# Weight blocks converted in pairs of 1024 columns, and a set order for VectorE's first work

## The chip, the cores and the metric

The kernel runs on one core of a Trainium2 chip. The metric is the device time of one execution in microseconds (us), the median of several runs. The engines of the core are named as in the profile: PE is TensorE (matrix products), DVE is VectorE, ACT is ScalarE, POOL is GpSimd, SP is SyncE, which only issues transfers here. PEld is the load of weights into TensorE.

## The reference, cut

```python
# attention: batch 8, 8 heads, 576 tokens, head dimension 64
kv = einsum('bhsd,bhse->bhde', k, v)
out = einsum('bhsd,bhde->bhse', q, kv)
rms = sqrt(mean(out * out, axis=-1, keepdims=True) + 1e-06)
x = (out / rms * g_norm)                  # -> 4608 tokens x 512
# first MLP, w_in 512 x 2048, w_out 2048 x 512
h = x @ w_in
x = (h * cos(h)) @ w_out
# second MLP, 512 -> 1024 -> 1024 -> 512
a, b = x @ w1, x @ w2
return ((a * b) @ w3) @ w_out
```

The weights come as float64 words, two 32-bit words a number. The kernel has to turn them into float32 itself.

## The kernel before, in words

Every product that needs full float32 accuracy is made of three products of rounded halves, hi x hi, hi x lo and lo x hi (`three`). So each operand is split: ScalarE copies it rounded (hi), VectorE or GpSimd subtracts that from the source (lo). That is `split`; a hi part always comes before its lo part, on another engine.

**The weights** come through the class `Chunk`, blocks of 128 x 512 numbers. A block is loaded as raw words on SP's queue (`load`), then `convert` makes float32 bits of it: one Abs on ScalarE (it only has to read the high words), and four VectorE operations: clamp (L139), shift and mask (L140), sign (L143) and the low word's bits (L146). Then `put` splits the result into the weight tile. A matrix step m of the first MLP needs one block of w_in (128 x 512, named i) and one of w_out (named u). `first_pairs` sets the order of these blocks and the buffers of their words: buffers of weights that are not there yet (tags wo8 to wo15), then bc. A load can only be issued when the buffer's last reader is done.

**The tokens** are cut into 16 units of 288 (two a batch entry) for attention, and into nine blocks t of 512 for the MLPs. `first_units` does units 0 and 1 by itself: for each of four head pairs p the product kv, the split of q, the product out, its square. A small matmul gathers the mean squares (`ms_first`), a Newton iteration on VectorE makes the inverse roots of all of them (L349 to L355: a start value and three rounds of three operations), a matmul with a unit matrix spreads them over the partitions (`spread`), and a multiply (L438) finishes o. Then `split_x` makes hi and lo parts of x of block t = 0.

All other units go through `unit_stage`, eleven stages s: loads of k, v and q, kv, out, mean square, then at s = 8 `emit_newton` (L349 to L355 on 128 x 18) and `emit_bc`: the inverse roots go to DRAM (rsd) and come back spread over the partitions (bc). At s = 10 `emit_x` multiplies (L383). Units 2 and 3, which make the x of block t = 1, are spread over the first seven steps by the table `quick`; their transfers go through GpSimd's queue (`queue`). They also need a trip through DRAM for the mean square (msd, then rsx).

**The steps.** The main loop runs over n; each step is a block t and a slice m of 128 of the 2048 hidden units. Steps 0 to 7 are t = 0 with m = 0 to 7, steps 8 to 23 are t = 1 with m = 0 to 15, steps 24 to 31 are t = 0 with m = 8 to 15, then t = 2 and so on. A step makes h (12 matmuls of 128 x 512, `emit_h`, h8 is that of step 8), then g = h cos h on ScalarE and VectorE (`g_first`: u, r, the rest; `g_rest`: sine, u x h, split), and two steps later g @ w_out is added up (`emit_w`, w5 is that of step 5). Two PSUM banks hold h; h of step n + 2 needs the bank of step n, which is free after the multiply u x h (L555).

**Who sets the order.** The code is written as a list per step, but a planner of the language orders each engine's instructions by a simulated timeline and puts in the waits. `tc.issue_after(op)` tells it not to place what follows before op. Every engine and each transfer queue then works strictly in the order that it was given.

Of the kernel before, what the change touches and what calls it, by code (L numbers as in the profile page):

```python
# [13 lines left out]
P = 128  # L14
EPS = 1e-6
# [19 lines left out]
def kernel(  # L35
# [47 lines left out]
    def wi_tile(m, name):  # L83
        return wpool.tile([P, 2, KD, P], F32R, tag=f"wi{m}", name=name)

    def wo_tile(m, name):
        return wpool.tile([P, 2, DM], F32R, tag=f"wo{m}", name=name)

# [25 lines left out]

    class Chunk:


        def __init__(self, name, src, tag, put):
            self.name, self.src, self.tag, self.put = name, src, tag, put

        def load(self):
            if self.tag == "stage":
                self.words = stage([P, CHUNK, 2], I32, f"{self.name}_w")
            elif self.tag == "bc":
                self.words = ap.tile([P, CHUNK, 2], I32, tag="bc", name=f"{self.name}_w")
            else:
                self.words = wpool.tile([P, CHUNK, 2], I32, tag=self.tag, name=f"{self.name}_w")
            word_loads.append(
                nc.sync.dma_start(out=self.words.rearrange("p n t -> p (n t)"), in_=self.src)
            )  # L130

        def convert(self):


            lo, hi = self.words[:, :, 0], self.words[:, :, 1]
            self.f = row(f"{self.name}_f")
            b = self.f.bitcast(I32)
            nc.scalar.activation(self.f, hi.bitcast(F32), AF.Abs)
            yield nc.vector.tensor_scalar(self.f, self.f, MOST, LEAST, ALU.min, ALU.max)  # L139
            yield nc.vector.tensor_scalar(  # L140
                b, b, 3, 0x3FFFFFF8, ALU.logical_shift_left, ALU.bitwise_and
            )
# [12 lines left out]
    def may_load():
        k = state["load"]
        if k >= len(chunks):
            return False
        tag = chunks[k].tag
        return tag == "stage" or last_words.get(tag, -1) < state["conv"]  # L160

    def prefetch(upto):
        while state["load"] < upto and may_load():
            c = chunks[state["load"]]
            c.load()
            last_words[c.tag] = state["load"]
            state["load"] += 1
# [27 lines left out]
    def put_w_in(m):  # L195
        def put(f):
            t = wi_tile(m, f"w_in{m}")
            split(t.rearrange("p i k f -> p i (k f)"), f)
            w_in[m] = t
        return put  # L200

    def put_w_out(m):
        def put(f):
            t = wo_tile(m, f"w_out{m}")
            split(t, f)
            w_out[m] = t
        return put

    def first_pairs():


        pairs = [(0, 0), (1, 0)]
        for m in range(2, NM):
            pairs += [(m, 0), (m - 2, 1)]
        pairs += [(NM - 2, 1), (NM - 1, 1)]
        free = list(range(NM // 2, NM))
        for m, s in pairs:
            if s == 1 and m in free:
                free.remove(m)
            tag = f"wo{free[0]}" if free else "bc"  # L220
            free = free[1:] + free[:1]
            nm, put = (("i", put_w_in), ("u", put_w_out))[s]
            src = w1pair[m, :, 2 * CHUNK * s:2 * CHUNK * (s + 1)]
            chunks.append(Chunk(f"{nm}{m}", src, tag, put(m)))

    first_pairs()
    n_first = len(chunks)
    for i in range(2 * NJ):
        chunks.append(Chunk(f"d{i}", w12w[i], "stage", put_later(("w12", i))))
    for c in range(NJ):  # L230
        chunks.append(Chunk(f"o{c}", wo2w[c], "stage", put_later(("wo2", c))))
    for half in range(2):
        for c in range(NJ):
            src = w3t[c, :, 2 * CHUNK * half:2 * CHUNK * (half + 1)]
            chunks.append(Chunk(f"a{half}{c}", src, "stage", put_later(("w3", half, c))))
# [53 lines left out]
    def load_q(u, p, tag=None):  # L289
        if tag:  # L290
            t = wpool.tile([P, HALF], F32, tag=tag, name=f"q_{u}_{p}")
# [55 lines left out]
    def newton(x, y, t):  # L347
# [41 lines left out]
    def first_units(spread):  # L389

        for p in range(NPAIR):
            emit_kv(0, p)
            evac_kv(0, p)
            for u in range(2):
# [3 lines left out]
                split(hl, q_raw.pop((u, p)), nc.vector)  # L398
# [17 lines left out]
                for k in range(NT3):  # L416
# [4 lines left out]
                    )  # L421
        n = 4 * NPAIR * NT3
        x, y, t = (row(f"rs_first_{i}")[0:T3, 0:n] for i in range(3))
        nc.vector.tensor_scalar(x, mst[0:T3, 0:n], EPS, HUGE, ALU.add, ALU.min)
        newton(x, y, t)
        for u in range(2):
            for p in range(NPAIR):
                ps = ps_acc.tile([P, 512], F32, tag=f"acc{p}", name=f"spread_{u}_{p}")
# [9 lines left out]
                nc.vector.tensor_tensor(o, o, ps[:, 0:HALF], ALU.mult)  # L438
# [102 lines left out]
    def g_first(n):  # L541
# [317 lines left out]
    if True:  # L859
# [8 lines left out]
        spread = wpool.tile([P, T3], F32, tag=f"wi{NM - 1}", name="spread")  # L868
# [19 lines left out]
        nc.vector.tensor_scalar(gneg, gneg, -1.0, None, ALU.mult)  # L888
        for p in range(NPAIR):
            for u in range(2):  # L890
                load_q(u, p, f"wi{4 + 2 * p + u}")
# [26 lines left out]
        for n in range(NS + 2):  # L918
# [7 lines left out]
            more = min(n_first, 9 + n + min(n, 8) // 2) - state["conv"] if n < NS else 0  # L926
# [12 lines left out]
            if n < NS:  # L939
                if more > 0:  # L940
                    put(more)
# [205 lines left out]
```

## Time and profile before

| | |
|---|---|
| time, median of 3 runs | 1544.08 us (1543.64 to 1544.95) |
| the profiled execution's own time | 1546.17 us |
| its span | 1544.40 us |
| mean granted clock of TensorE | 0.993 |
| busy, PE / DVE / ACT / POOL | 1500.9 / 924.8 / 697.5 / 371.4 us |
| share of the chain that ended last | PE 81%, DMA 5%, DVE 3%, POOL 3%, ACT 2% |

The span is the time between the first and the last instruction of the profiled execution; its own time has 1.77 us around that, and lies 2.09 us above the median of the runs. The busy times may overlap between engines. A busy time of one instruction is longer than the distance to the next one, since an engine starts the next before the last is written. In the timelines, square brackets give the idle time of the engine before the instruction and what ended it.

### The profile page before, as it was taken

To read this page: it belongs to the slowest core of one execution; us is meant where nothing else is said; L and a number is where in the kernel's file an instruction comes from. 1 tells how busy PE (TensorE), PEld (TensorE's weight loads), DVE (VectorE), ACT (ScalarE), POOL (GpSimd) and SP (SyncE) were. 2 spreads that over 40 slices of the span, in tenths; PEclk is the share of its full clock that TensorE was granted. 3 is DMA by queue.
4 is the path that set the end of the run, shared out by engine and by line. 5 is a ranking of instruction groups with operands and counts; after the bars stand their busy time and mean duration, and the time that the engine had idled before them with its cause. 6 is when DMAs were issued, how large, how long until landed. Compare 5 with 4: busy or idle time off the path is not lost.

```text
span 1544.4 us, 20537 instructions
## 1 busy us (share of the span) xinstructions
PE 1500.9 (97%) x7616; PEld 1272.0 (82%) x7616; DVE 924.8 (60%) x1714; ACT 697.5 (45%) x1405; POOL 371.4 (24%) x301
## 2 busy tenths in 40 slices
PE   6799999999999999999999998999999999999998
PEld 6577888788787787878887887999998998999997
DVE  3998844566566666766666447644544456545453
ACT  4667654444454454444534335433433334333331
POOL 1111010120010211101102006454444417344420
PEclk9799999999999999999999999999999999999999
DMA  8655120433333425234222015121102313223312
GB/s 288 218 158 159 43 71 7 150 111 110 113 97 97 146 97 153 87 108 132 88 73 92 11 40 192 42 82 69 69 28 82 110 59 113 78 93 123 123 62 75
DMA packets 81956, 156.26 MB, mean 101 GB/s; under 512 B 11600, under 2 KB 37376, under 8 KB 81856
## 3 DMA queue, kind: packets, MB, share of 16 engines
q1 hardware_dynamic: 80240, 150.18, 30.3%
q0 software_dynamic: 1616, 4.78, 1.0%
q8 instruction: 59, 0.97, 0.3%
q14 instruction: 41, 0.34, 0.1%
HBM read 113.77 MB, written 41.15 MB: 100 GB/s over the span
## 4 chain that ended last, share of the span: by engine, by line
PE 81%; DMA 5%; DVE 3%; POOL 3%; ACT 2%; issue 2%; SPq 0%; ACTq 0%; POOLq 0%; DVEq 0%
PE X L762 11%; PE h L529 8%; PE x L531 8%; PE x L530 8%; PE h L531 8%; PE h L530 8%; PE x L529 8%; PE V L762 5%; PE o L529 4%; PE o L530 4%; PE o L531 4%; PE Y L762 3%; POOL xc L112 2%; DMA x2r<-x_all 2%; PE kv L269 1%
## 5 line engine op out<-in xcount | busy, mean ns | idle before, releaser
L762 PE MATMUL X<-xc,w 128*128 128x384 f32 x1152 | 230.0, 337 | 6.6 <-ACT s L770 5.9
L531 PE MATMUL x<-g,w_out 128*128 128x512 f32 x576 | 227.6, 395 | 0.0
L530 PE MATMUL x<-g,w_out 128*128 128x512 f32 x576 | 227.1, 394 | 0.0
L529 PE MATMUL h<-x,w_in 128*128 128x512 f32 x544 | 216.3, 398 | 5.1 <-DVE u L555 3.4
L762 PEld LDWEIGHTS X<-xc,w 128*128 128x128 f32 x1152 | 204.0, 188 | 19.9 <-ACT s L770 9.9
L530 PE MATMUL h<-x,w_in 128*128 128x512 f32 x544 | 215.1, 395 | 1.8 <-DVE x L112 1.8
L531 PE MATMUL h<-x,w_in 128*128 128x512 f32 x544 | 215.0, 395 | 0.0
L529 PE MATMUL x<-g,w_out 128*128 128x512 f32 x576 | 212.7, 392 | 1.1 <-ACT g L110 0.6
L112 POOL TENSOR_TENSOR xc<-x2r,xc 128x768 fp32r<-128x768 f32 x70 | 134.6, 1930 | 225.2 <-ACT xc L110 225.2
L543 ACT ACTIVATE u<-h 128x512 f32<-128x512 f32 x144 | 86.2, 598 | 157.4 <-PE h L531 153.8
L554 ACT ACTIVATE u<-u 128x512 f32<-128x512 f32 x144 | 91.0, 632 | 121.6 <-DVE u L550 106.7
L112 DVE TENSOR_TENSOR g<-u,g 128x512 fp32r<-128x512 f32 x144 | 104.4, 725 | 64.6 <-ACT g L110 64.4
L110 ACT ACTIVATE g<-u 128x512 fp32r<-128x512 f32 x144 | 90.9, 632 | 109.1 <-DVE u L555 86.3
L112 POOL TENSOR_TENSOR qhl<-q,qhl 128x288 fp32r<-128x288 f32 x48 | 42.3, 884 | 397.7 <-ACT qhl L110 317.8
L529 PEld LDWEIGHTS h<-x,w_in 128*128 128x128 f32 x544 | 103.1, 190 | 33.0 <-DVE u L555 8.0
L530 PEld LDWEIGHTS x<-g,w_out 128*128 128x128 f32 x576 | 108.6, 189 | 24.6 <-DVE rs L353 0.5
L529 PEld LDWEIGHTS x<-g,w_out 128*128 128x128 f32 x576 | 107.6, 188 | 25.2 <-DVE x2s L576 0.8
L531 PEld LDWEIGHTS x<-g,w_out 128*128 128x128 f32 x576 | 108.8, 189 | 23.0
L555 DVE TENSOR_TENSOR u<-u,h 128x512 f32<-128x512 f32 x144 | 98.7, 685 | 47.3 <-ACT u L554 46.9
L549 DVE TENSOR_SCALAR r<-u 128x512 f32<-128x512 f32 x112 | 50.7, 453 | 127.3 <-ACT u L543 127.2
L770 ACT ACTIVATE s<-X 128x384 f32<-128x384 f32 x144 | 65.9, 487 | 133.6 <-PE X L762 133.2
L530 PEld LDWEIGHTS h<-x,w_in 128*128 128x128 f32 x544 | 103.1, 190 | 24.4 <-DVE x L112 2.5
(183 smaller groups left out, 2646.9 us busy)
## 6 DMA issues: line engine op xcount, KB each, us to landing
x2r<-x_all SPq DMA_DIRECT2D x44, 384.0 KB
kvraw<-in_kv_main_dram SPq DMA_DIRECT2D x28, 512.0 KB
x_all<-x2s SPq DMA_DIRECT2D x36, 256.0 KB
part<-o SPq DMA_DIRECT2D x36, 256.0 KB
part<-part SPq DMA_DIRECT2D x36, 256.0 KB
out_dram<-part SPq DMA_DIRECT2D x36, 256.0 KB
i_w<-in_w1pair_dram SPq DMA_DIRECT2D x16, 512.0 KB
u_w<-in_w1pair_dram SPq DMA_DIRECT2D x16, 512.0 KB
```

What stands on the lines that cost most here:

```text
L110: nc.scalar.activation(dst[:, 0], src, AF.Copy)
L112: lo_engine.tensor_tensor(dst[:, 1], src, f32(dst[:, 0]), ALU.subtract)
L269: nc.tensor.matmul(ps[d, 0:D], k[:, d], v[:, d], start=i == 0, stop=i == NC)
L529: nc.tensor.matmul(ps, w[0], x[0], start=first, stop=False)
L530: nc.tensor.matmul(ps, w[0], x[1], start=False, stop=False)
L531: nc.tensor.matmul(ps, w[1], x[0], start=False, stop=last)
L543: nc.scalar.activation(u, h_ps[n], AF.Identity, bias=0.25, scale=INV_2PI)
L549: nc.vector.tensor_scalar(r, u, ROUND, ROUND, ALU.add, ALU.subtract)
L554: nc.scalar.activation(u, u, AF.Sin, scale=-TWO_PI_DOWN)
L555: nc.vector.tensor_tensor(u, u, h_ps.pop(n), ALU.mult)
L762: nc.tensor.matmul(ps, w[:, self.i, a, k], x[:, b, k], start=first and k == 0 and n == 0, stop=last and k == 1 and n == 2, skip_group_chec ...
L770: nc.scalar.activation(s, ps, AF.Copy)
```

## The change

Blocks of w_in and w_out of one m are handled together, as a `Pair`: one load of 1 MB (1024 numbers of 64 bits a partition), one Abs, four VectorE operations of 1024 columns, one hi and one lo operation. The result is written into the high words of the raw buffer itself instead of a buffer of its own. The words of the first eight pairs lie where the weights of pairs 8 to 15 will be and all eight loads stand right behind those of q. Pair 15 is converted in two halves through the bc buffers.

`first_units` sets an order with `behind`: the four VectorE operations of pair 0 stand between the q splits, then Newton comes in one run, then pair 0 is split, then for each p the spread, the multiply, the split of x and the operations of pair 1. The quick units stand behind pair 1 (`marks[2]`), and the conversion of pair n + 2 in step n behind the last u of g (`marks[-1]`). In steps 7, 9 and so on to 21 the pairs 8 to 15 follow.

```diff
+    def bits(f, words, at):
+        lo, hi = words[..., 0], words[..., 1]
+        b, at = f.bitcast(I32), at.bitcast(I32)
+        nc.scalar.activation(f, hi.bitcast(F32), AF.Abs)
+        yield nc.vector.tensor_scalar(f, f, MOST, LEAST, ALU.min, ALU.max)
+        yield nc.vector.tensor_scalar(
+            b, b, 3, 0x3FFFFFF8, ALU.logical_shift_left, ALU.bitwise_and
+        )
+        yield nc.vector.scalar_tensor_tensor(
+            at, hi, -0x40000000, b, ALU.bitwise_and, ALU.bitwise_or
+        )
+        yield nc.vector.scalar_tensor_tensor(
+            at, lo, 29, at, ALU.logical_shift_right, ALU.bitwise_or
+        )
...
+    class Pair:
...
+        def load(self):
+            m = self.m
+            at = m + NM // 2 if m < NM // 2 else m + 1
+            self.raw = wpool.tile([P, 2 * CHUNK, 2], I32, tag=f"w{at}", name=f"words_{m}")
+            nc.sync.dma_start(out=self.raw.rearrange("p n t -> p (n t)"), in_=w1pair[m])
+
+        def convert(self):
+            f = wpool.tile([P, 2, CHUNK], F32, tag=f"w{self.m}", name=f"bits_{self.m}")
+            words = self.raw.rearrange("p (s n) t -> p s n t", s=2)
+            self.f = words[..., 1].bitcast(F32)
+            yield from bits(f, words, self.f)
...
+        def put(self):
+            t = self.tile()
+            nc.scalar.activation(t[:, :, 0], self.f, AF.Copy)
+            return nc.vector.tensor_tensor(
+                t[:, :, 1], self.f, f32(t[:, :, 0]), ALU.subtract
+            )
...
     def first_units(spread):
+        first = pairs[0].convert()
+        step = None
         for p in range(NPAIR):
...
-                split(hl, q_raw.pop((u, p)), nc.vector)
+                with behind(step):
+                    split(hl, q_raw.pop((u, p)), nc.vector)
...
+            for _ in range((0, 2, 1, 1)[p]):
+                step = next(first)
         n = 4 * NPAIR * NT3
         x, y, t = (row(f"rs_first_{i}")[0:T3, 0:n] for i in range(3))
-        nc.vector.tensor_scalar(x, mst[0:T3, 0:n], EPS, HUGE, ALU.add, ALU.min)
-        newton(x, y, t)
-        for u in range(2):
-            for p in range(NPAIR):
-                ps = ps_acc.tile([P, 512], F32, tag=f"acc{p}", name=f"spread_{u}_{p}")
+        with behind(step):
+            nc.vector.tensor_scalar(x, mst[0:T3, 0:n], EPS, HUGE, ALU.add, ALU.min)
+        marks.append(newton(x, y, t))
+        with behind(marks[1]):
+            pairs[0].put()
+        second = pairs[1].convert()
+        step = None
+        for p in range(NPAIR):
+            for u in range(2):
+                ps = ps_acc.tile([P, 512], F32, tag=f"acc{(2 * p + u) % 4}", name=f"spread_{u}_{p}")
...
-                nc.vector.tensor_tensor(o, o, ps[:, 0:HALF], ALU.mult)
+                with behind(step):
+                    step = nc.vector.tensor_tensor(o, o, ps[:, 0:HALF], ALU.mult)
+            split_x(0, p)
+            with behind(step):
+                for _ in range((0, 1, 1, 2)[p]):
+                    step = next(second)
+        with behind(step):
+            marks.append(pairs[1].put())
+
+    def behind(op):
+        return tc.issue_after(op.ins) if op is not None else nullcontext()
...
+        for m in range(NM // 2):
+            pairs[m].load()
         first_units(spread)
-        for c in range(KD):
-            split_x(0, c)
-        for _ in range(4):
-            prefetch(state["conv"] + 8)
-            convert(2)
-            put(2)
+        pairs[NM // 2].load()
...
+            pair = None
+            if n < HM - 2:
+                pair = pairs[n + 2]
+            elif n >= HM - 1 and n % 2 == 1 and HM + (n - HM + 1) // 2 < NM:
+                pair = pairs[HM + (n - HM + 1) // 2]
             if n < NS:
...
-                if more > 0:
-                    prefetch(min(state["conv"] + 8, n_first))
-                    convert(more)
+                if pair is not None:
+                    with behind(marks[-1]):
+                        for _ in pair.convert():
+                            pass
                 emit_h(n)
...
-            for u, s in quick.get(n, ()):
-                one = [unit_stage(u, s)]
-                for i in range(4):
-                    run(one, i)
+            with behind(marks[2]):
+                for u, s in quick.get(n, ()):
+                    one = [unit_stage(u, s)]
+                    for i in range(4):
+                        run(one, i)
```

The order of the instructions that the planner makes of this, at three places. The numbers of lines below are those of each kernel's own file.

ScalarE, the hi parts of x of block t = 0 (`x`, the copies from o) and the first operations on raw words (`i_f`, `u_f` and `bits`, the Abs). Before:

```order
L138 ACTIVATE u_f<-u_w 128x512
L110 ACTIVATE kv_80<-kv_2_634 64x64
L320 ACTIVATE sq_1_656<-out_1_649 128x288
L321 ACTIVATE o_592<-out_1_649,gneg 128x288
L110 ACTIVATE qhl_3_678<-q_3_632 128x288
L110 ACTIVATE kv_80<-kv_2_634 64x64
L110 ACTIVATE w_in_450<-i_f 128x512
L110 ACTIVATE x_383<-o_151 128x288
L138 ACTIVATE i_f<-i_w 128x512
L110 ACTIVATE w_out_453<-u_f 128x512
L110 ACTIVATE x_383<-o_151 128x288 x2
```

Now (words_134 are those of pair 2, words_136 of pair 3 and so on to words_144 of pair 7):

```order
L114 ACTIVATE bits_432<-words_134 128x1024
L413 ACTIVATE sq_3_301<-out_3_297 128x288
L414 ACTIVATE o_161<-out_3_297,gneg 128x288
L413 ACTIVATE sq_3_314<-out_3_310 128x288
L414 ACTIVATE o_176<-out_3_310,gneg 128x288
L114 ACTIVATE bits_524<-words_136 128x1024
L114 ACTIVATE bits_619<-words_138 128x1024
L114 ACTIVATE bits_701<-words_140 128x1024
L104 ACTIVATE x_354<-o_161 128x288
L104 ACTIVATE x_354<-o_176 128x224
L114 ACTIVATE bits_769<-words_142 128x1024
L104 ACTIVATE x_354<-o_161 128x288
```

The Abs of pairs 3, 4 and 5 stand ahead of the first hi part of x, those of pairs 6 and 7 between the others. Before, the operations of unit 2 stood there.

VectorE, where unit 2's bc is multiplied and unit 3's Newton runs (L383, now L386: o by bc; L355, now L357: the last operation of a Newton round, rs_3 is unit 3's). Before:

```order
L383 TENSOR_TENSOR o_592<-o_592,bc_922 128x288
L146 SCALAR_TENSOR_TENSOR u_f<-u_w,u_f 128x512
L112 TENSOR_TENSOR g_827<-u_805,g_827 128x512
L383 TENSOR_TENSOR o_592<-o_592,bc_922 128x288 x3
L355 SCALAR_TENSOR_TENSOR rs_3_996<-rs_3_997,rs_3_996 128x18
L143 SCALAR_TENSOR_TENSOR i_f<-i_w,i_f 128x512
```

Now:

```order
L355 TENSOR_TENSOR rs_3_903<-rsx_847,rs_3_902 128x18
L386 TENSOR_TENSOR o_520<-o_520,bc_830 128x288 x4
L356 SCALAR_TENSOR_TENSOR rs_3_903<-rs_3_903,rs_3_902 128x18
L106 TENSOR_TENSOR g_1013<-u_978,g_1013 128x512
L106 TENSOR_TENSOR kv_81<-kv_3_1585,kv_81 64x64
L106 TENSOR_TENSOR x_998<-o_520,x_998 128x288
L357 SCALAR_TENSOR_TENSOR rs_3_902<-rs_3_903,rs_3_902 128x18
L106 TENSOR_TENSOR x_998<-o_520,x_998 128x288 x3
L106 TENSOR_TENSOR kv_81<-kv_3_1585,kv_81 64x64
L386 TENSOR_TENSOR o_697<-o_697,bc_917 128x288 x4
L367 TENSOR_SCALAR rsx_1743<-rsx_1743 128x18
L106 TENSOR_TENSOR x_998<-o_697,x_998 128x160
```

Before, the multiplies by unit 2's bc stood ahead of the end of the first of unit 3's three Newton rounds, and 27 rows of VectorE later came the last operation of the last round. Now they stand ahead of the last two operations of the last round, and unit 3's own multiplies follow ten instructions later.

TensorE, at the first matmuls of h8 (L529 to L531, now L555 to L557, are `three`; w_in_428 and w_335 are the weights of m = 0, w_425 those of m = 1, w_888 of m = 7; L310 and L312 are attention's out). Before:

```order
L310 MATMUL out_1_1736<-qhl_1_1674,kv_79 128x288
L311 MATMUL out_1_1736<-qhl_1_1674,kv_79 128x288
L312 MATMUL out_1_1736<-qhl_1_1674,kv_79 128x288
L269 MATMUL kv_3_1778<-kvraw_3_1681 64x64 x8
L269 MATMUL kv_3_1778<-kvrest_1485 64x64 x2
L529 MATMUL h_1166<-x_1112,w_in_428 128x512
L530 MATMUL x_0_0_723<-g_1066,w_out_984 128x512
L531 MATMUL x_0_0_723<-g_1066,w_out_984 128x512
L530 MATMUL x_0_1_727<-g_1066,w_out_984 128x512
```

Now:

```order
L556 MATMUL x_0_3_655<-g_1013,w_888 128x512
L557 MATMUL x_0_3_655<-g_1013,w_888 128x512
L312 MATMUL out_3_1662<-qhl_3_1624,kv_81 128x288
...
L313 MATMUL out_1_1831<-qhl_1_1792,kv_79 128x288
L314 MATMUL out_1_1831<-qhl_1_1792,kv_79 128x288
L313 MATMUL out_2_1903<-qhl_2_1867,kv_80 128x288
L314 MATMUL out_2_1903<-qhl_2_1867,kv_80 128x288
L555 MATMUL h_1040<-x_998,w_335 128x512
L555 MATMUL h_1069<-x_998,w_425 128x512
L312 MATMUL out_3_1960<-qhl_3_1912,kv_81 128x288
L331 MATMUL ms_2010<-sq_0_1796,sel 32x288
```

Before, h8 came ahead of w7 and of most products of units 4 and 5. Now w7 and all but one of these products come first, and h8 and h9 are made in turns.

## Rows read from the trace of the kernel before

**Rows 1.** The page, part 1: busy time and share of each engine.

```profile
PE 1500.9 (97%) x7616; PEld 1272.0 (82%) x7616; DVE 924.8 (60%) x1714; ACT 697.5 (45%) x1405; POOL 371.4 (24%) x301
```

**Rows 2.** Window 160 to 400: length, busy PE, PEld, DVE, ACT, POOL, clock, DMA, GB/s.

```profile
160.00:400.00 240.00, 240.00 (x1192) 194.35 (x1191) 147.51 (x286) 121.19 (x241) 23.57 (x26) 1.00 0.28 86
```

**Rows 3.** The DMA view of 0 to 160 us: GB/s in slices of 4 us.

```profile
GB/s 163 278 329 255 310 384 401 220 200 356 292 187 344 305 205 252 165 92 138 145 137 193 218 115 83 215 120 58 258 82 291 55 244 220 136 185 180 59 77 0
```

**Rows 4.** Timelines of SP's queue and of POOL: start, length, engine, line.

```profile
16.48 0.71 SPq L129 DMA_DIRECT2D u_w<-in_w1pair_dram  x1
33.78 0.33 SPq L129 DMA_DIRECT2D i_w<-in_w1pair_dram  x1
...
25.79 0.54 POOL L294 DMA_DIRECT2D q<-in_qt_dram  x1
```

**Rows 5.** Timeline of VectorE, 24 to 40 us.

```profile
27.50 0.20 DVE L424 TENSOR_SCALAR rs_first<-ms_first 96x48 f32<-96x48 f32 x1 [3.49 <-PE ms_first L418]
...
33.01 0.69 DVE L146 SCALAR_TENSOR_TENSOR i_f<-i_w,i_f 128x512 int32<-128x512 int32 x1
33.61 0.69 DVE L143 SCALAR_TENSOR_TENSOR i_f<-i_w,i_f 128x512 int32<-128x512 int32 x1
...
37.47 0.20 DVE L355 SCALAR_TENSOR_TENSOR rs_first<-rs_first,rs_first 96x48 f32<-96x48 f32 x1
37.59 0.41 DVE L140 TENSOR_SCALAR i_f<-i_f 128x512 int32<-128x512 int32 x1
37.92 0.45 DVE L112 TENSOR_TENSOR qhl<-q,qhl 128x288 fp32r<-128x288 f32 x1
```

**Rows 6.** Timeline of ScalarE: the first two Abs.

```profile
26.34 1.22 ACT L138 ACTIVATE i_f<-i_w 128x512 f32<-128x512 f32 x2
```

**Rows 7.** Timeline of TensorE: the first matmuls of h0.

```profile
50.88 1.22 PE L529 MATMUL h<-x,w_in 128*128 128x512 f32 x2 [1.65 <-ACT x L110]
```

**Rows 8.** The trips of units 2 and 3: timelines of VectorE and POOL, and bc's view.

```profile
81.84 0.59 POOL L373 DMA_DIRECT2D rsd<-rs  x1 [2.12 <-DVE rs L355]
92.17 0.46 DVE L383 TENSOR_TENSOR o<-o,bc 128x288 f32<-128x288 f32 x1 [2.75 <-DMA bc<-rsd]
106.44 0.83 DVE L355 SCALAR_TENSOR_TENSOR rs<-rs,rs 128x18 f32<-128x18 f32 x1
110.19 1.23 POOL L377 DMA_DIRECT2D bc<-rsd  x2 [2.02 <-DMA rsd<-rs]
116.01 1.55 DVE L383 TENSOR_TENSOR o<-o,bc 128x288 f32<-128x288 f32 x4
...
DMA to landing us min/median/max: 4.2/5.4/7.0
```

**Rows 9.** Window 27.5 to 121.2, columns as in rows 2.

```profile
27.50:121.20 93.70, 76.53 (x482) 56.89 (x483) 84.65 (x209) 61.45 (x139) 16.53 (x24) 0.89 0.62 193
```

**Rows 10.** Timeline of TensorE, 118 to 148 us.

```profile
118.14 0.64 PE L529 MATMUL h<-x,w_in 128*128 128x512 f32 x1
118.59 0.63 PE L530 MATMUL x<-g,w_out 128*128 128x512 f32 x1
...
126.71 0.39 PE L530 MATMUL h<-x,w_in 128*128 128x512 f32 x1
126.94 0.39 PE L531 MATMUL h<-x,w_in 128*128 128x512 f32 x1
...
127.96 1.08 PE L529 MATMUL x<-g,w_out 128*128 128x512 f32 x4
...
132.93 0.50 PE L529 MATMUL h<-x,w_in 128*128 128x512 f32 x1 [0.21 <-DVE u L555]
...
138.38 0.50 PE L529 MATMUL x<-g,w_out 128*128 128x512 f32 x1 [0.50 <-DVE x2s L576]
...
147.95 0.50 PE L529 MATMUL h<-x,w_in 128*128 128x512 f32 x1 [0.33 <-DVE u L555]
```

**Rows 11.** VectorE's groups, 0 to 160 us: busy us, mean ns, idle before.

```profile
L547 DVE SCALAR_TENSOR_TENSOR u<-r,u 128x512 f32<-128x512 f32 x14 | 9.6, 684 | 1.4 <-ACT r L546 1.4
L143 DVE SCALAR_TENSOR_TENSOR i_f<-i_w,i_f 128x512 int32<-128x512 int32 x14 | 9.6, 682 | 0.0
```

More of the change, by code (lines that the diff above doesn't have):

```diff
@@ L81 @@
     gneg = const.tile([P, 1], F32, name="gneg")
[L83 to L87, printed above, removed]
     def row(name):
@@ new lines, with __init__, tile @@
+    w_in, w_out, wo2 = {}, {}, {}
+    w3 = {}
+    later = {}
+    class Pair:
+        def __init__(self, m):
+            self.m = m
+        def load(self):
[8 more added lines that the diff above has]
+            yield from bits(f, words, self.f)
+        def tile(self):
+            m = self.m
+            t = wpool.tile([P, 2, 2, CHUNK], F32R, tag=f"w{m}", name=f"w_{m}")
+            w_in[m] = t[:, 0].rearrange("p i (k f) -> p i k f", k=KD)
+            w_out[m] = t[:, 1]
+            return t
+        def put(self):
[4 more added lines that the diff above has]
+            )
@@ new lines, with load, convert, put @@
+    class LastPair(Pair):
+        def load(self):
+            pass
+        def convert(self):
+            m, t = self.m, self.tile()
+            for k in range(2):
+                raw = ap.tile([P, CHUNK, 2], I32, tag="bc", name=f"words_{m}_{k}")
+                src = w1pair[m, :, 2 * CHUNK * k:2 * CHUNK * (k + 1)]
+                nc.sync.dma_start(out=raw.rearrange("p n t -> p (n t)"), in_=src)
+                f = row(f"f_{m}_{k}")
+                yield from bits(f, raw, f)
+                split(t[:, k], f, nc.vector)
+        def put(self):
+            pass
@@ L115, with __init__ @@
+    pairs = [Pair(m) for m in range(NM - 1)] + [LastPair(NM - 1)]
     class Chunk:
-        def __init__(self, name, src, tag, put):
-            self.name, self.src, self.tag, self.put = name, src, tag, put
+        def __init__(self, name, src, put):
+            self.name, self.src, self.put = name, src, put
         def load(self):
[L122 to L130, printed above, removed]
+            self.words = stage([P, CHUNK, 2], I32, f"{self.name}_w")
+            nc.sync.dma_start(out=self.words.rearrange("p n t -> p (n t)"), in_=self.src)
@@ L162, in prefetch @@
     def prefetch(upto):
[L163 to L166, printed above, removed]
+        while state["load"] < min(upto, len(chunks)):
+            chunks[state["load"]].load()
             state["load"] += 1
@@ L193, in put_later @@
         return put
[L195 to L227, printed above, removed]
     for i in range(2 * NJ):
-        chunks.append(Chunk(f"d{i}", w12w[i], "stage", put_later(("w12", i))))
+        chunks.append(Chunk(f"d{i}", w12w[i], put_later(("w12", i))))
     for c in range(NJ):
-        chunks.append(Chunk(f"o{c}", wo2w[c], "stage", put_later(("wo2", c))))
+        chunks.append(Chunk(f"o{c}", wo2w[c], put_later(("wo2", c))))
     for half in range(2):
@@ L287, with load_q @@
     q_hl = {}
-    def load_q(u, p, tag=None):
-        if tag:
-            t = wpool.tile([P, HALF], F32, tag=tag, name=f"q_{u}_{p}")
+    def load_q(u, p, home=None):
+        if home is not None:
+            t = home[:, p]
         else:
@@ L867 @@
             nc.gpsimd.memset(sel[D * h:D * h + D, h:h + 1], 1.0 / D)
-        spread = wpool.tile([P, T3], F32, tag=f"wi{NM - 1}", name="spread")
+        spread = const.tile([P, T3], F32, name="spread")
         nc.gpsimd.memset(spread, 0.0)
@@ L939 @@
             if n < NS:
-                if more > 0:
-                    put(more)
+                if pair is not None:
+                    pair.put()
+                    if pair.m < NM // 2:
+                        pairs[pair.m + NM // 2 - 1].load()
                 after = steps[n + 1][0] if last and n + 1 < NS else t
```

46 lines of the change are left out of this document (15 added, 31 removed).

## The prediction

> **What bounds the kernel now.** I read the page's busy shares first: TensorE (PE) is busy for 97% of the span [rows 1], so only its idle and slow stretches can be won or lost. The windows say where they are: from 160 us on it is busy 240.00 of 240 us [rows 2]. So every late edit (fewer VectorE and ScalarE instructions from step 10 on, the last pair in the bc buffers) is worth nothing: TensorE hides it, and without that cover it would still be a saving. The case is decided in the first 135 us, and by one date: when the second block's x is ready. The timeline of TensorE shows it: the first matmul of h8 at 118.14, then matmuls 0.45 us apart, the clock's lower level, later 0.23 apart; h8 and h9 end at 127.2, w7 runs from 127.96, h10 starts at 132.93 with 0.21 idle; later, to 160 us, it is idle for 0.50 and 0.33, 0.83 in all [rows 10].
>
> That x hangs on a chain: mean square of unit 2, Newton on VectorE, a trip through DRAM (rsd, bc), multiply; the same for unit 3. From the first Newton operation at 27.50 [rows 5] to the end of that x at 121.2 VectorE is busy 84.65 of 93.7 us [rows 9]. So VectorE and the trips set the date together. One profiled execution gives all durations; its time is 1546.17 us, 1.77 over its span and 2.09 over the median of the runs. I work out a difference and lay it on the median, 1544.08.
>
> **Prices.** VectorE, start to start [rows 5]: 0.60 us for a two-input operation of 512 columns (33.01 to 33.61), 0.33 for a one-input one (37.59 to 37.92), 0.12 for a small one (37.47 to 37.59). Four of 288 columns with two inputs took 1.55 together where one takes 0.45, so (1.55 - 0.45)/3 = 0.37 each [rows 8]. The slope from 288 to 512 is 0.23/224 = 1.03 ns a column, so 1024 columns cost 0.60 + 512 x 0.00103 = 1.13. The fixed part is 0.37 - 0.30 = 0.07; by it a one-input one of 1024 costs 0.07 + 2 x 0.26 = 0.59, say 0.60. No row has that width: the ends are no saving at all (0.66, 1.20) and the whole 288-column fixed part saved twice. A pair of blocks cost 2 x (2 x 0.33 + 3 x 0.60) = 4.9; now 2 x 0.60 + 3 x 1.13 = 4.6. So 0.3 us a pair, about 2.5 us before the second block's x: little. ScalarE gains no more, and is not full.
>
> **Part 1: the first block's x.** Newton in one run ends about 5 us earlier than the interleaved one (37.47 [rows 5]): pair 0's four operations between the q splits (3.5 us, partly in gaps) delay its start from 27.5 to about 30, and eleven small ones at less than 0.3 end by 33. But the order of ScalarE now has the Abs of pairs 3, 4 and 5 ahead of the first hi part of x, and pairs 6 and 7 among the rest. The engine works in that order, so x waits for words_5. All eight loads stand on SP's queue behind q with nothing to wait for; before, the next load came at 33.78 because it waited for VectorE's last read of a buffer. By 28 us the queues moved 2120 GB/s x 4 us = 8.48 MB, the sum of the first seven 4-us figures [rows 3]. Up to words_5 SP has 2048 + 256 + 1152 + 6144 KB = 9.83 MB, and POOL's queue 1568 KB = 1.61 MB by its last load at 25.79 [rows 4]. The 2.96 MB left take 7.4 us at the 401 GB/s of 24 to 28 us [rows 3]: 35.4, some 36 with the completion. Two Abs of 512 took 1.22 us [rows 6], so one of 1024 takes no more, and the hi part of x at most half of that: VectorE gets x at 38. Ends: 34 (POOL's share comes later) and 40.
>
> The Trainium skill (DMA: Bandwidth & Descriptors, "Where 436 GB/s comes from") says that between HBM and SBUF the limit of one core at the HBM, about 358 GB/s, binds. By that figure the 2.96 MB would take 8.3 us and the forecast would be 0.9 us later, 1548.6. The trace moved 401 GB/s in that window [rows 3], so the measurement decides.
>
> From 38, 11 operations of 288 columns, 4 of 224 and pair 1's five make 11 x 0.37 + 4 x 0.30 + 4.6 = 9.9 us: 47.9. The hi copy of pair 1 ahead of its lo part (1.2) and four rounds of spread matmuls and multiplies make it 52; ends 48 and 53. Before, h0 began at 50.88 [rows 7] and got its last x at 59; now h0 is over by 50 and h1 by 55. That is the gain, some 7 us for the first block.
>
> **Part 2: VectorE up to Newton of unit 2.** From the end of pair 1 to the last Newton operation of unit 2 the new order has 14 one-input and 18 two-input operations of 1024, 20 two-input ones of 512, 8 of 288 and 24 small ones: 14 x 0.60 + 18 x 1.13 + 20 x 0.60 + 8 x 0.37 + 24 x 0.13 = 46.8 us. How long it waits in between no row tells. At these prices the 200 rows of before that fill 27.5 to 121.2 make 82.0 of 93.7 us: 14% on top [rows 9]. Ends: none, and 14%. I take half, 7%, since quick units and conversions now stand behind each other in a set order and fewer results are asked for at once: 50.1 us, so Newton ends at 102.1. Before, unit 2's was sent off at 81.84 [rows 8]: the change puts the quick units behind pair 1 and the conversions ahead of them, and gives 20 us of the lead away.
>
> **Part 3: two trips in a row.** Before, unit 2's bc came at 92.17, long before unit 3's Newton ended (106.44 + 0.83 = 107.27); only the second trip was on the path. It took 116.01 - 107.27 = 8.7 us; the first, from rsd to the multiply, 10.3 [rows 8]. The least is 2.9 to bc's issue, 0.6 to its second half and 4.2 to land: 7.7. In the new order the four multiplies by bc of unit 2 stand ahead of unit 3's last two Newton operations. So unit 3 can't be sent off until unit 2 has come back, and the 7 us of VectorE work between them lie within the trip. The sum: 102.1 + 8.3 + 2.8 (four multiplies, g of n = 7, a split, the last Newton operation) + 8.3 + 1.8 (four multiplies, a small one, the first split of 160) = 123.3. This is T0, the first quarter of x complete.
>
> **Part 4: TensorE behind T0.** In the new order w6, w7 and all of unit 4's and three of unit 5's products stand ahead of h8 and h9, which come in turns. So TensorE has nothing else behind T0: 24 matmuls at 0.23 = 5.5, plus 2.0 for about ten of them at the lower clock after the wait, plus 0.5 until the other quarters are there. h8 and h9 then end together, and h10 needs the bank of h8: two ScalarE passes (about 1.1) and six VectorE operations (six times 0.60, 3.6), with the end of the last 5.3 in all, and again 2.0 of slow clock: T0 + 15.3. In exchange, what before stood behind h10 is done: the rest of unit 5 (two products and its mean square, about 1.3 at the durations of such matmuls) and the idle 0.83, so before stands at 132.93 + 2.13 = 135.06. The change pays where T0 is before 135.06 - 15.3 = 119.7. With 123.3 it loses 3.6 us: **1547.7**.
>
> **The other edits.** The spread tile in const, kv and q in other buffers: no wait shows at them before, nothing is taken. Half as many word loads spare SP 16 issues of about 0.7 us [rows 4], beside its waits: nothing. TensorE's instructions are the same.
>
> **Rivals.** What a measurement can tell from no change is about 0.2%, 3.1 us.
>
> A, the other side: faster, 0.25. If ScalarE's wait for the words is short (x at 35) and VectorE runs without stalls, as long runs of wide operations let it, Newton of unit 2 ends at 48 + 46.8 = 94.8 to 96; with 2 x 7.7 + 4.6 = 20 us behind it T0 is 115 to 116 and the time 1539.4 to 1540.4. It decides at 96.5 for Newton's end. For it speaks the 7 us by which the first block comes earlier; against it the 14% of before [rows 9].
>
> B, no change, 0.30: pair 1 at 50, stalls of 3 to 5%, trips at 7.7 to 8: T0 between 117 and 122.8, its middle 120, 1544.4. The earlier start and the second trip cancel.
>
> C, far slower, 0.08: stalls at the full 14% and the first trip at 10.3, with POOL's lo parts of q of units 4 and 5 in its row between the two trips: 52 + 53.4 + 10.3 + 2.8 + 8.7 + 1.8 = 129.0, 1553.4.
>
> D, the change costs what it doesn't seem to, 0.04: two operations a pair now write every second word in place. Reading so is free (682 ns against 684 [rows 11]); writing so has no row. At half speed it is 2 x 1.06 a pair, for seven pairs 15 us: 1563.
>
> **Numbers.** The forecast's own case (T0 from 122.5 to 127, 1546.9 to 1551.4) has 0.33, of which 0.01 counts as no change. With A, B, C and D that gives faster 0.25, same 0.31, slower 0.44. The range goes from A with pair 1 somewhat before 48, 1538.5, to C, 1553.5; outside lie D and the far ends of A and C, some 0.13.
>
> **What would show it.** Right: a wait of VectorE or ScalarE for a words load near 36 to 38; h0's first matmul at 39 to 41 and h1 done by 56; Newton of unit 2 sent off at 101 to 104; a VectorE wait at each of the two multiplies by bc; h8 and h9 done near 131, and a wait of TensorE of 4 to 5 us ahead of h10. Wrong: bc of unit 2 back before 104, h8 begun before 117, or two-input operations of 1024 columns above 1.4 us.

## The result and the profile after

The changed kernel takes 1565.02 us (median of 4 runs, 1564.61 to 1567.45), the kernel before in the same comparison 1544.51: a ratio of 1.0132 (95% interval 1.0115 to 1.015), some 20 us slower. The forecast was a loss of 3.6 us. The profiled execution has a span of 1563.0 us, 18.6 more than before. The page, part 1:

```profile
PE 1517.0 (97%) x7616; PEld 1271.9 (81%) x7616; DVE 921.4 (59%) x1639; ACT 694.0 (44%) x1375; POOL 370.9 (24%) x301
```

Against [rows 1] TensorE is *busy* for 16.1 us more, with the same number of matmuls (x7616), and idle for only (1563.0 - 1517.0) - (1544.4 - 1500.9) = 2.5 us more. So most of the loss is no wait at all. Two groups of the page show it, first after, then before (busy us, mean ns of one | idle us):

```profile
L556 PE MATMUL x<-g,w 128*128 128x512 f32 x576 | 229.4, 398 | 1.1 <-DVE g L106 1.1
L556 PE MATMUL h<-x,w 128*128 128x512 f32 x544 | 217.9, 400 | 0.0
```

```profile
L530 PE MATMUL x<-g,w_out 128*128 128x512 f32 x576 | 227.1, 394 | 0.0
L530 PE MATMUL h<-x,w_in 128*128 128x512 f32 x544 | 215.1, 395 | 1.8 <-DVE x L112 1.8
```

Each matmul of the first MLP takes 4 to 5 ns longer. The timeline of TensorE after, far behind the start, shows the distances from one start to the next (the spacing):

```profile
399.97 0.39 PE L556 MATMUL x<-g,w 128*128 128x512 f32 x1
400.20 0.40 PE L557 MATMUL x<-g,w 128*128 128x512 f32 x1
400.44 0.39 PE L555 MATMUL x<-g,w 128*128 128x512 f32 x1
400.67 0.40 PE L556 MATMUL x<-g,w 128*128 128x512 f32 x1
400.90 0.39 PE L557 MATMUL x<-g,w 128*128 128x512 f32 x1
```

Four distances make 0.93 us, 0.233 each at a granted clock of 1.00. Over some 1,300 to 1,400 neighbouring starts of each kind between 160 and 920 us the mean is 0.2334 after and 0.2289 to 0.2290 before; single spacings lie between 0.225 and 0.237. There are 144 steps of 24 such matmuls, 3456; times 0.0044 that is 15 us, an estimate.

The rest lies where the prediction looked. Here is the chain to the second block's x in the timeline of VectorE after (the 48.39 row is pair 1's lo part, 104.98 the last Newton operation of unit 2, 118.00 that of unit 3; L367 is the first operation on a unit's rsx, L386 the multiply by bc):

```profile
48.39 1.23 DVE L161 TENSOR_TENSOR w<-words,w 128x1024 fp32r<-128x1024 f32 x1 [1.20 <-ACT w L160]
49.54 0.69 DVE L115 TENSOR_SCALAR bits<-bits 128x1024 f32<-128x1024 f32 x1
...
98.97 0.17 DVE L356 SCALAR_TENSOR_TENSOR rs<-rs,rs 128x18 f32<-128x18 f32 x1
103.57 0.18 DVE L367 TENSOR_SCALAR rsx<-rsx 128x18 f32<-128x18 f32 x1 [4.43 <-DMA rsx<-msd]
...
104.98 0.17 DVE L357 SCALAR_TENSOR_TENSOR rs<-rs,rs 128x18 f32<-128x18 f32 x1
...
114.85 1.56 DVE L386 TENSOR_TENSOR o<-o,bc 128x288 f32<-128x288 f32 x4 [1.37 <-DMA bc<-rsd]
...
118.00 0.17 DVE L357 SCALAR_TENSOR_TENSOR rs<-rs,rs 128x18 f32<-128x18 f32 x1
...
126.00 1.56 DVE L386 TENSOR_TENSOR o<-o,bc 128x288 f32<-128x288 f32 x4 [6.47 <-DMA bc<-rsd]
...
128.37 0.31 DVE L106 TENSOR_TENSOR x<-o,x 128x160 fp32r<-128x160 f32 x1
```

The two waits for bc are there as foreseen; before there was one, at unit 2's first multiply [rows 8]. A third wait was not foreseen: VectorE stands 4.43 us at unit 3's rsx while unit 2's last Newton operation, whose input was ready at about 99.1, stands behind it. So three trips lie in a row, that of unit 3's mean square first. ScalarE, which copies the mean square out of PSUM (L340), and GpSimd, which issues the trip, show its course:

```profile
90.27 0.38 ACT L340 ACTIVATE ms_sb<-ms 128x288 f32<-128x288 f32 x1
```

```profile
89.40 3.51 POOL L106 TENSOR_TENSOR qhl<-q,qhl 128x288 fp32r<-128x288 f32 x1 [5.30 <-DVE rs L355]
92.85 1.18 POOL L345 DMA_DIRECT2D msd<-ms_sb  x2
98.97 0.58 POOL L346 DMA_DIRECT2D rsx<-msd  x1 [4.93 <-DMA msd<-ms_sb]
105.44 0.56 POOL L376 DMA_DIRECT2D rsd<-rs  x1 [5.90 <-DVE rs L351]
...
135.03 0.81 POOL L106 TENSOR_TENSOR qhl<-q,qhl 128x288 fp32r<-128x288 f32 x1 [4.18 <-ACT qhl L104]
```

A subtraction that takes 0.81 us where VectorE idles (131.7 to 137.7) took 3.51 beside VectorE's two-input operations of 1024 columns, and the msd transfers stood behind it. The mean square was there at 90.65 and left at 92.85, so the subtraction accounts for at most 2.2 of the 4.43 us; the trip itself, from 92.85 to 103.57, took 10.7. The Trainium skill (SBUF — State Buffer, "Who interferes with whom") says that a VectorE instruction with two SBUF inputs contends with a GpSimd one that reads SBUF; the 3.51 us agree.

TensorE at h10, after: its first matmul, then the lower clock (a granted clock of 0.55 from 141.58 to 145.29), by the last two lines 0.42 us apart.

```profile
141.58 0.50 PE L555 MATMUL h<-x,w 128*128 128x512 f32 x1 [4.86 <-DVE u L583]
141.92 0.59 PE L556 MATMUL h<-x,w 128*128 128x512 f32 x1
142.31 0.63 PE L557 MATMUL h<-x,w 128*128 128x512 f32 x1
142.73 0.63 PE L555 MATMUL h<-x,w 128*128 128x512 f32 x1
```

Before, h10 started at 132.93 [rows 10], 8.65 us earlier.

### The profile page after: what moved, and what is told of

Its sections match the earlier page's. It is cut to its first block, busy times and chain, and to the rows that moved or that the text cites. A ratio compares the mean times of both kernels' runs of the same rounds, so it can differ in the third digit from the quotient of the medians.

```text
span 1563.0 us, 20358 instructions
## 1 busy us (share of the span) xinstructions
PE 1517.0 (97%) x7616; PEld 1271.9 (81%) x7616; DVE 921.4 (59%) x1639; ACT 694.0 (44%) x1375; POOL 370.9 (24%) x301
## 4 chain that ended last, share of the span: by engine, by line
PE 82%; DMA 6%; POOL 4%; DVE 3%; ACT 2%; issue 2%; SPq 1%; ACTq 0%; DVEq 0%; POOLq 0%
PE X L790 10%; PE h L555 8%; PE h L556 8%; PE h L557 8%; PE x L557 8%; PE x L556 8%; PE x L555 8%; PE V L790 5%; PE o L555 4%; PE o L556 4%; PE o L557 4%; PE Y L790 2%; POOL xc L106 2%; DMA x2r<-x_all 2%; DMA words<-in_w1pair_dram 2%
## 5 line engine op out<-in xcount | busy, mean ns | idle before, releaser
L556 PE MATMUL x<-g,w 128*128 128x512 f32 x576 | 229.4, 398 | 1.1 <-DVE g L106 1.1
L557 PE MATMUL x<-g,w 128*128 128x512 f32 x576 | 229.2, 398 | 0.0
L555 PE MATMUL h<-x,w 128*128 128x512 f32 x544 | 219.2, 404 | 9.7 <-DVE u L583 5.0
L556 PE MATMUL h<-x,w 128*128 128x512 f32 x544 | 217.9, 400 | 0.0
L557 PE MATMUL h<-x,w 128*128 128x512 f32 x544 | 217.3, 399 | 0.0
L555 PE MATMUL x<-g,w 128*128 128x512 f32 x576 | 210.5, 397 | 2.5 <-ACT g L104 2.5
L555 PEld LDWEIGHTS h<-x,w 128*128 128x128 f32 x544 | 103.5, 191 | 39.6 <-DVE u L583 8.7
L556 PEld LDWEIGHTS x<-g,w 128*128 128x128 f32 x576 | 108.8, 189 | 27.9 <-DVE g L106 1.9
L555 PEld LDWEIGHTS x<-g,w 128*128 128x128 f32 x576 | 107.6, 188 | 28.1 <-ACT g L104 2.9
L557 PEld LDWEIGHTS x<-g,w 128*128 128x128 f32 x576 | 108.8, 189 | 25.8
L557 PEld LDWEIGHTS h<-x,w 128*128 128x128 f32 x544 | 103.6, 191 | 24.5 <-issue 0.5
```

Of the source, the lines that this page charges most:

```text
L555: nc.tensor.matmul(ps, w[0], x[0], start=first, stop=False)
L556: nc.tensor.matmul(ps, w[0], x[1], start=False, stop=False)
L557: nc.tensor.matmul(ps, w[1], x[0], start=False, stop=last)
```

## The experiments: why every matmul is slower

From 153 us on TensorE's matmuls come in the order of before. What else can change a matmul's pace? Two theories. A: addresses. The change puts the spread tile, 384 bytes a partition, among the constants, so everything above them, x and g with it, lies 384 bytes higher (x at 31392 instead of 31008, as the program assigns it; the weights, which are laid out from the other end, stay at 98272 plus multiples of 4096). B: the weights' new tiles of 8 KB, or the loads.

**e1**: the changed kernel, orders untouched.

```diff
-        spread = const.tile([P, T3], F32, name="spread")
+        spread = ap.tile([P, T3], F32, tag="bc", name="spread")
```

> The changed kernel with one edit: the 384-byte spread tile lies in the bc buffer of attention instead of the constants, so x and g lie at the addresses of before; every engine's order is that of the changed kernel. Theory A (addresses: the spread tile moved x and g by 384 bytes and each 128x512 matmul of the first MLP takes 0.2333 instead of 0.2289 us, 3328 of them, 14.6 us): spacing back at 0.229, time about 1565.0 - 14.6 = 1550.4 us (1549 to 1552). Theory B (the pairs' weight tiles of 8 KB, or the loads, slow the matmuls): spacing stays at 0.233, time stays at 1565.

Measured: 1551.76 us (1549.09 to 1553.79), before beside it 1545.38, ratio 1.0038 (1.0023 to 1.0053). Mean spacing 0.2291 for h, 0.2289 for w. Its page:

```profile
L556 PE MATMUL x<-g,w 128*128 128x512 f32 x576 | 227.1, 394 | 1.1 <-DVE g L106 1.1
```

That is the 394 ns of before. Theory A holds, B falls: 1565.02 - 1551.76 = 13.3 us of the loss are the place of one small tile. (The expectation's 3328 matmuls should be 3456.)

**e2**, **e3**, **e4**, **e8**, **e9**: the kernel before with an unused tile of N bytes, which GpSimd clears once, and no other edit; x and g move by N, which is 384, 512, 128, 256 and 32.

```diff
+    pad = const.tile([P, N // 4], F32, name="pad")
...
+        nc.gpsimd.memset(pad, 0.0)
```

> The kernel before with one edit: an unused tile of 384 bytes a partition among the constants, cleared once by GpSimd; all orders are those of before, x and g lie 384 bytes higher. Theory A: spacing 0.233 us, time about 1544.5 + 14.6 = 1559.1 us. Theory B: 0.229 and 1544.5, no change.

> As e2 with 512 bytes. Theory A, if what matters repeats every 512 bytes or less (the weights lie at a fixed offset in steps of 512): 1544.5 us and 0.229. Theory A with a longer period: some other spacing, up to 1559. Theory B: 1544.5.

> As e2 with 128 bytes. Theory A says only that it may differ: between 1544.5 (offset as good as before) and 1559 or more. Theory B: 1544.5.

> As e2 with 256 bytes. If what matters repeats every 256 bytes: spacing 0.2289 and about 1544.5 us. If every 512: some other spacing, 0.2333 or more.

> As e2 with 32 bytes. If only the distance in steps of 128 bytes counts: 0.2289 and 1544.5 us. If finer steps count: another spacing, better or worse.

e2's page, where nothing but an unread tile differs from before:

```profile
PE 1516.3 (97%) x7616; PEld 1272.7 (82%) x7616; DVE 926.7 (59%) x1714; ACT 697.7 (45%) x1405; POOL 368.9 (24%) x302
...
L532 PE MATMUL x<-g,w_out 128*128 128x512 f32 x576 | 229.5, 398 | 0.0
```

A matmul reads a moving operand (x or g, 512 columns) and the weights that were loaded before. Is it the moving operand's own address, or its distance to the weights? **e10** puts an unused tile of 128 bytes above the weights, which then lie 128 bytes lower; **e11** does that and e4's shift of x and g:

```diff
             if n == NM + HM:
                 load["alone"] = False
+                wpad = wpool.tile([P, 32], F32, name="wpad")
+                nc.gpsimd.memset(wpad, 0.0)
```

> The kernel before with an unused tile of 128 bytes above the weights: all weight tiles lie 128 bytes lower, x and g where they were; all orders are those of before. If the distance between a matmul's moving operand (x, g) and its weights decides: spacing 0.2333 us and about 1559 us, as in e4. If the moving operand's own address decides: 0.2289 and 1544.5.

> e4 and e10 together: x and g 128 bytes higher, the weights 128 lower, so their distance is changed by 256 bytes. If the distance decides (and repeats every 256 bytes, as e8 says of x and g): 0.2289 us and about 1544.5. If the moving operand's own address decides: 0.2333 and 1559.

**e13** gives x and g different distances in one execution (the tile among the constants has 64 bytes, `mpad` in x's and g's pool 128, between them):

```diff
+        mpad = m1.tile([P, 32], F32, name="mpad")
+        nc.gpsimd.memset(mpad, 0.0)
```

> The kernel before with x 64 bytes higher and g 192 bytes higher (an unused tile of 64 bytes among the constants and one of 128 between x and g); all orders are those of before. The distance theory says that the matmuls of h (moving x) and those of w (moving g) may now have spacings of their own, each 0.229 or 0.233 us; a third level below 0.229 would make a faster kernel. If both are slow, the good place is a narrow one: about 1559 us; if both are fast, 1544.5.

e13's page, the two kinds side by side:

```profile
L532 PE MATMUL x<-g,w_out 128*128 128x512 f32 x576 | 226.6, 393 | 0.0
...
L532 PE MATMUL h<-x,w_in 128*128 128x512 f32 x544 | 216.4, 398 | 0.0
```

All results, the distance being moving operand minus weights, modulo 256 bytes (means of spacings worked out as above; the times of e8, e9, e10, e11 and e13 are of one run each):

| kernel | distance | spacing h / w, us | time, us |
|---|---|---|---|
| before | 64 | 0.2290 / 0.2289 | 1544.5 |
| e9, x and g +32 | 96 | 0.2332 / 0.2332 | 1561.67 |
| e4, +128 | 192 | 0.2335 / 0.2334 | 1557.86 |
| e8, +256 | 64 | 0.2291 / 0.2289 | 1544.14 |
| e2, +384 | 192 | 0.2334 / 0.2334 | 1559.85 |
| e3, +512 | 64 | 0.2291 / 0.2290 | 1544.77 |
| e10, weights -128 | 192 | 0.2333 / 0.2333 | 1558.80 |
| e11, both | 64 | 0.2292 / 0.2289 | 1545.06 |
| e13, x +64, g +192 | 128 and 0 | 0.2326 / 0.2286 | 1548.27 |
| changed | 192 | 0.2334 / 0.2334 | 1565.02 |
| e1 | 64 | 0.2291 / 0.2289 | 1551.76 |

The distance decides, not the own address: e4 and e11 have x and g at the same addresses, e10 and e11 the weights, and only e11 is fast. Over the shifts tried it repeats every 256 bytes: 0 and 64 are fast, 96, 128 and 192 slow. e3 and e8 carry the same unused tile as e2 and lose nothing, so its clearing costs nothing. A mean below 0.2286 was not seen for x and g.

A third kind of matmul bears it out: the 864 of 128x512 in the second MLP (`wchl` moving, `ab` as weights), whose distance changes with the shifts of x and g but not with e10's shift of the weights. Their mean spacing is 0.2300 at 0 and 64 (before, e1, e3, e8, e10, e13), 0.2323 at 192 (changed, e2, e4, e11) and 0.2335 at 96 (e9). In e11 they are slow while those of x and g are fast. Its page:

```profile
L532 PE MATMUL x<-g,w_out 128*128 128x512 f32 x576 | 227.1, 394 | 0.0
...
L532 PE MATMUL o<-wchl,ab 128*128 128x512 f32 x288 | 110.5, 394 | 0.0
```

And e10's, where it is the other way round:

```profile
L531 PE MATMUL x<-g,w_out 128*128 128x512 f32 x576 | 229.4, 398 | 0.0
...
L531 PE MATMUL o<-wchl,ab 128*128 128x512 f32 x288 | 109.4, 390 | 0.0
```

By these means some 864 x 0.0023 = 2.0 us of the loss are theirs, an estimate, and they are part of e1's 13.3 us. With the 15 above it makes 17, within e2's interval (ratio 1.0096, 1.0072 to 1.012, so 11 to 18.5 us).

## The experiments: the order up to the second block's x

What is left of the loss is e1's 0.38%, about 6 us. Theory C: the trips that stand in a row in VectorE's order. Theory D: something else. **e5** is e1 with two orders, unit 3's Newton behind unit 2's and unit 2's multiplies behind unit 3's Newton (`ends[u]` is a unit's last Newton operation):

```diff
-        nc.vector.tensor_scalar(x, x, EPS, HUGE, ALU.add, ALU.min)
-        newton(x, y, t)
+        with behind(ends.get(u - 1) if u == 3 else None):
+            nc.vector.tensor_scalar(x, x, EPS, HUGE, ALU.add, ALU.min)
+        ends[u] = newton(x, y, t)
...
-        engine.tensor_tensor(o, o, bc[u][:, p, :], ALU.mult)
+        with behind(ends[3] if u == 2 else None):
+            engine.tensor_tensor(o, o, bc[u][:, p, :], ALU.mult)
...
-            5: [(2, 10), (3, 8)], 6: [(3, 10)],
+            5: [(3, 8), (2, 10)], 6: [(3, 10)],
```

> e1 with two orders added: unit 3's Newton only behind the last Newton operation of unit 2, and unit 2's multiplies by bc only behind unit 3's last Newton operation. Theory C (in the changed order VectorE stands at the first operation on unit 3's rsx until 101.4 us while unit 2's last Newton operation waits behind it, and unit 3's Newton then waits for unit 2's bc: three trips in a row): unit 2's rsd leaves at about 98 instead of 103.3, no wait at unit 2's multiplies, unit 3's rsd at about 111 to 112 instead of 116.2, x of the second block some 4 us earlier, time about 1551.8 - 4 = 1548 us. Theory D (the loss of e1 is elsewhere, VectorE's amount of work or the gap behind h8 and h9 alone): within 1 us of e1.

Measured: 1546.74 us against 1545.43 before, ratio 1.0002 (0.9988 to 1.0016), 5.0 us below e1. The time speaks for C and against D, but the path changed only in part:

```profile
101.30 0.17 DVE L358 SCALAR_TENSOR_TENSOR rs<-rs,rs 128x18 f32<-128x18 f32 x1
...
113.26 0.16 DVE L358 SCALAR_TENSOR_TENSOR rs<-rs,rs 128x18 f32<-128x18 f32 x1
113.37 1.56 DVE L389 TENSOR_TENSOR o<-o,bc 128x288 f32<-128x288 f32 x4
...
123.59 1.56 DVE L389 TENSOR_TENSOR o<-o,bc 128x288 f32<-128x288 f32 x4 [6.58 <-DMA bc<-rsd]
```

Unit 2's multiplies no longer wait, but its Newton ended at 101.5 instead of about 98, and the second trip took 10.2 us, from 113.4 to 123.6; the first quarter of x is ready at 125.4 instead of e1's 126.4, 1.0 us earlier and not 4. h10 in e1 and in e5:

```profile
139.30 0.79 PE L555 MATMUL h<-x,w 128*128 128x512 f32 x1 [4.87 <-DVE u L583]
```

```profile
137.52 0.51 PE L558 MATMUL h<-x,w 128*128 128x512 f32 x1 [3.46 <-DVE u L586]
```

That is 1.8 us, and the profiled executions themselves are 2.3 apart (1549.09 and 1546.76). Where the rest of the 5.0 between the medians comes from, no trace shows: e5 doesn't show C's mechanism. **e7** also takes pair 8 out of the way:

```diff
-                    with behind(marks[-1]):
+                    with behind(ends[3] if n == 7 else marks[-1]):
                         for _ in pair.convert():
```

> e5 with the conversion of pair 8 set behind unit 3's last Newton operation, so that unit 3's Newton has little work beside it. Theory C: unit 3's rsd leaves at 105 to 107, its bc is back at 115 to 116, x of the second block at about 117.5, 9 us before e1: about 1543 us, the time of the kernel before or 1 to 2 us better. Theory D: within 1 us of e1, 1551.

Measured: 1551.35 us, ratio 1.0035 (1.0021 to 1.0049); a miss for C, and the 1551 that D had named. Unit 3's rsd left at 107.53 and x was there at 122.3, 4 us before e1, but the time is e1's. GpSimd, VectorE and TensorE say what took it back:

```profile
114.80 1.24 POOL L382 DMA_DIRECT2D bc<-rsd  x2 [1.72 <-DVE o L389]
```

```profile
128.50 0.18 DVE L369 TENSOR_SCALAR rsx<-rsx 128x18 f32<-128x18 f32 x1 [5.44 <-DMA rsx<-msd]
...
137.33 0.68 DVE L586 TENSOR_TENSOR u<-u,h 128x512 f32<-128x512 f32 x1
```

```profile
138.06 0.80 PE L558 MATMUL h<-x,w 128*128 128x512 f32 x1 [6.69 <-DVE u L586]
```

There is one bc buffer, so unit 3's transfer waits for unit 2's multiplies; and behind x VectorE stands at unit 4's rsx and converts pair 9 before it frees h8's bank. **e12** takes up both (`gends[n]` is the multiply u x h of step n; pair 14's load moves to step 9):

```diff
...
+        if u == 3:
+            t = wpool.tile([P, NPAIR, HALF], F32, tag="w15", name=f"bc_{u}")
...
+        with behind(ends.get(u - 1) if u == 3 else gends[9] if u in (4, 5) else None):
...
+                if pair is not None and n >= HM:
+                    with behind(gends[n]):
+                        for _ in pair.convert():
+                            pass
+                        pair.put()
```

> e7 with three edits: unit 3's bc has a buffer of its own (that of pair 14's words, loaded later), the conversions of pair 9 and later stand behind the multiply u x h of their step, and the Newtons of units 4 and 5 behind that of step 9. In e7 unit 3's bc could only be issued at 114.8, when unit 2's multiplies had read the one bc buffer, and h10 then waited 6.7 us for VectorE, which stood at unit 4's Newton and converted pair 9 first. Theory C with these two: unit 3's bc leaves at about 110, x of the second block at about 117.5, h10 starts at 127 to 129 instead of 138, time 1539 to 1542 us, faster than both kernels. If the order after h9 is not what counts: 1546 to 1551, as e5 and e7.

Measured: 1546.45 us (1543.21 to 1553.18, 12 runs) against 1545.09, ratio 1.0016 (1.0002 to 1.003). VectorE and TensorE:

```profile
117.52 1.56 DVE L393 TENSOR_TENSOR o<-o,bc 128x288 f32<-128x288 f32 x4 [2.18 <-DMA bc<-rsd]
119.00 1.63 DVE L106 TENSOR_TENSOR x<-o,x 128x160 fp32r<-128x160 f32 x4
```

```profile
131.57 0.80 PE L562 MATMUL h<-x,w 128*128 128x512 f32 x1 [2.35 <-DVE u L590]
```

x comes 7 us before e1's and h10 starts 7.7 us before (139.30 there), still 2.6 us later than expected. The median falls by 5.3, the ratio by 0.0022 (3.4 us), and its interval overlaps with e1's. Together these waits do cost time, as C says. But 1539 to 1542 was expected, and 1546.45 lies in the range that was named for the case that the order after h9 isn't what counts. The profiled execution, 1543.21, is the fastest of the twelve, so its trace doesn't show what the slower ones lose; that stays open. Of the 6 us the cause is thus shown in part only: with all the edits together 3 to 5 come back, and how much each wait holds, e5 and e7 don't tell apart. No version tried here beats the kernel before.

## Why the prediction was wrong

**The step that failed** is in "The other edits": "The spread tile in const, kv and q in other buffers: no wait shows at them before, nothing is taken." The term was put at nothing. The tile moved x and g against the weights, and 3456 matmuls came 4.4 ns further apart: 13.3 us (e1), 14.5 us when done alone to the kernel before (e2, 1559.85 - 1545.38). An address shows in no wait, so looking for waits could not find it. "TensorE's instructions are the same" was true of their number and kind, and not of the places of their operands.

**The rest, forecast as 3.6 us,** measured about 6 (e1's 0.38%). Its terms:
- Prices: two-input operations of 1024 columns last 1.22 us and come 1.13 to 1.15 apart (48.39 to 49.54 above), foreseen 1.13. Rival D, which named 1563, is refuted: the operation that writes every second word (L119) takes as long as the one that doesn't (L161). That its time came out near is chance. VectorE's groups after, 0 to 160 us:

```profile
L119 DVE SCALAR_TENSOR_TENSOR words<-words,bits 128x1024 int32<-128x1024 int32 x11 | 13.4, 1218 | 0.1
L161 DVE TENSOR_TENSOR w<-words,w 128x1024 fp32r<-128x1024 f32 x11 | 13.4, 1215 | 1.8 <-ACT w L160 1.8
```

- Part 1: pair 1 ended at 49.6, not 52; h0 began at 38.98 and h1 was over at 54.4, as foreseen. The words came earlier than thought: ScalarE's wait for those of pair 5 ended at 32.09, not at 36 (its timeline and the DMA view of 0 to 160 us, slices of 4 us, both after):

```profile
32.09 1.17 ACT L114 ACTIVATE bits<-words 128x1024 f32<-128x1024 f32 x1 [1.66 <-DMA words<-in_w1pair_dram]
```

```profile
GB/s 168 335 272 317 397 430 422 417 411 225 2 269 194 395 113 196 281 313 256 122 61 304 123 159 348 205 2 259 124 209 115 92 193 37 39 199 70 2 0 0
```

  From 16 to 36 us the queues moved 397 to 430 GB/s, without the pause of before [rows 3]. The Trainium skill (DMA: Bandwidth & Descriptors, "Where 436 GB/s comes from") has about 358 GB/s as the limit that binds between HBM and SBUF; these slices lie above it, more clearly than those of before.
- Part 2: Newton of unit 2 ended at 105.15, foreseen 102.1. The sum of work was nearly right: from 49.54 to 105.15 VectorE was busy for 49.9 of 55.6 us, against 46.8 of work and 50.1 with waits. The missing term is the 4.43 us at unit 3's rsx, which stood ahead of unit 2's last Newton operation in the new order; I followed the trips of rsd and bc and not that of msd and rsx.
- Part 3: two trips in a row, as foreseen: 114.85 - 105.15 = 9.7 and 126.00 - 118.17 = 7.8 instead of 8.3 each. T0 came at 128.7, in e1 at 126.4, foreseen 123.3. Rival C had 129.0, but by stalls of 14% and a first trip of 10.3, not by the wait at rsx; that it comes so near is chance.
- Part 4: h10 began 12.9 us behind T0, 4.86 of them a wait just ahead of it, and then about nine matmuls ran at the lower clock (1.8 us more): together 14.7, close to the 15.3. By that formula e1's T0 of 126.4 costs 126.4 - 119.7 = 6.7 us; 5.9 were measured (0.0038 x 1545.4). As a rule for other orders it doesn't hold: e5's 125.4 would cost 5.7, and 0.3 were measured (0.0002 x 1545.4); e7 reached 122.3 and lost 5.4, since its wait ahead of h10 grew to 6.69.

Of what the prediction said would show it right, the wait for words near 36 to 38 was missing, Newton of unit 2 was sent off at 105.44 instead of 101 to 104, and h8 and h9 were done at 136 instead of 131; the two waits for bc and that ahead of h10 were there. None of its signs of being wrong appeared, since nothing in either list looked at TensorE's pace.

## What to carry over

When a change adds, drops or moves a buffer, list the addresses of the operands of the hottest instruction before and after; a few hundred bytes among the constants cost more here than the whole new schedule. Compare first the busy time of the engine that bounds the kernel, then its waits: 16.1 us more busy with as many matmuls pointed at the pace at once. And on an engine that works in order, look at every instruction that stands ahead of the critical one, not only at those of its own chain.

## What the runs showed that I had not expected

The mean spacing of the fp32r matmuls of 128x512 with x and g fell into two groups, 0.2286 to 0.2292 and 0.2326 to 0.2335 us, by the distance between moving operand and weights modulo 256 bytes (0 and 64 fast; 96, 128 and 192 slow; others were not tried), even within one execution (e13). Those of the second MLP follow the same distances with levels of their own. Why is not shown. And a GpSimd subtraction of 288 columns took 3.51 us instead of 0.81 beside VectorE operations with two inputs; this was read from traces and not tried by itself. The width of 1024 isn't needed: in e10, with the orders of before, one took 2.95 us beside a row of operations of 512 columns.
